# Attention followed by a token-mixing layer on one core: x transposed by DMA in six batches, attention in half groups, and products of zeros while TensorE waits

## The chip, the cores and the metric

One core of a Trainium2 chip. The metric is the device time of one execution in microseconds (us). Most executions of one kernel agree within 0.3%. Below, a "batch" is one of the eight batch entries that the program computes in a row.

Engines in the profile: PE is TensorE's matmuls, PEld its weight loads, DVE is VectorE, ACT is ScalarE, POOL is GpSimd, SP is SyncE. SPq and ACTq are the DMA queues that SP and ACT issue to. PEclk is the granted TensorE clock as a share of full speed.

## The reference, cut to what matters

```python
# q: 8 batches x 16 heads x 384 x 64;  k, v: 8 x 4 x 384 x 64  (4 query heads share one k/v head)
scores = (q @ k.T) / 8 ; attn = softmax(scores)
x   = (attn @ v), heads side by side              # per batch 384 x 1024
wq  = x @ w_q ; wk = x @ w_k                      # 384 x 64 each
W   = (wq @ wk.T) / 8                             # 384 x 384
out = relu(W @ x) @ w_out                         # 384 x 1024 per batch, float32
```

## The kernel before, cut to what the change touches

All matmuls are bf16. Per batch there are 18 score pairs (each followed by one exp of 128x1024 on ACT), six attention groups of two halves, and then a chain: x is transposed to xT, xT times (w_q, w_k) gives wT ("wqk", 8 products of 384 columns), `wk_tr`, `mix_c` (wk times x), `mix_m` (wq times that, relu), and 48 products of the output projection, `po`. A scheduler in Python, with a clock for each engine (`clk`) and times at which things are thought to be ready (`ready`), decides when the program is built in which order the instructions are emitted. On the chip each engine runs them in that fixed order. So where an estimate in `ready` is wrong, an engine stands and waits.

```python
def load(b):                                     # a batch's loads, float32, 2.36 MB, on SP's queue
    ...
    else:
        ld(kraw, k, 0, 4)                        # 384 KB
        ld(qraw, q, 0, half)                     # 768 KB
        ld(qraw, q, half, Hq)                    # 768 KB
        ld(vraw, v, 0, 4)                        # 384 KB

def attend(b, g):                                # one attention group, both halves: two banks
    ...
    ready["X", b, c, kp] = done
    if b > 0 and c < C - 1 and kp == KP - 1:     # C = 3: pieces 0 and 1 of x go by DMA,
        x_tr_dma(b, c)

def x_tr_dma(b, c):
    x_open(b)
    xn = xnats[b].rearrange("p c h d -> p c (h d)")
    nc.sync.dma_start_transpose(out=xTs[b][:, :, c, :], in_=xn[:, c, :])
    ready["T", b, c] = when(("X", b, c, 0), ("X", b, c, 1)) + 4500   # assumed landing, ns

def x_tr(b, c):                                  # piece 2, and all of batch 0: 8 transposes on TensorE
    ...
    for dc in range(DC):
        nc.tensor.transpose(out=ps[:, dc, :], in_=xn[:, c, dc * P:(dc + 1) * P], identity=ident)
    nc.vector.tensor_copy(out=xTs[b][:, :, c, :], in_=ps)

def after_s(b, s):                               # what is started after score pair s of batch b
    n = b + 1
    if b == 0 or n >= B:
        return
    if s == 0:
        load(n)                                  # the next batch's loads
    elif s == 5:
        cast(n)
        start_tr(n)
    elif s in (9, 11, 13, 15):
        tr_dma(n, (s - 9) // 2)                  # K and Q of the next batch, transposed by DMA
```

Scores run about one batch ahead of the chain. That is why the loads of batch b+2 are issued about when x of batch b is complete: they hang on the first score pair of batch b+1.

The softmax here doesn't subtract the row's maximum and nothing guards it: scores larger than these inputs give would overflow.

## Time and profile before

| | before |
|---|---|
| time, median of 3 runs | 223.95 us (223.94 to 224.87) |
| span of the profiled run | 221.7 us |
| busy: PE, DVE, ACT, POOL | 92%, 65%, 64%, 24% |
| first projection product starts | 44.94 us |
| last matmul ends, then tail | 217.44 us, 4.3 us |

The page's busy line, its groups, the windows, the timelines and the landings are in the prediction below. A group's columns are line, engine, operation, output and inputs, sizes, count; then busy us and mean ns of one; then the idle time of the engine just before these instructions.

```profile
PE 87%; ACT 4%; DVE 4%; issue 2%; DMA 1%; ACTq 0%
...
L328 PE MATMUL bank<-xT,wqk_sb 128*128 128x384 bf16 x64 | 11.8, 327 | 0.0
```

The chain runs over TensorE for 87% of the span and over DMA for 1%. The step wqk, which reads xT, never waits (0.0).

### The profile page before, as it was taken

Reading aid. Unit: us, or ns where it says so; the run is one execution under the profiler, and the core shown is the slowest. Engines: PE = TensorE matmul, PEld = TensorE weight load, DVE = VectorE, ACT = ScalarE, POOL = GpSimd, SP = SyncE. Lnnn points to the kernel's source line nnn. Section 1 sums busy time; section 2 is a strip of 40 time slices with the busy share of each in tenths; the row PEclk is TensorE's granted clock in tenths of the full one; section 3 lists DMA queues with packets and bytes.
Section 4 is the critical chain, followed back from the end, with each engine's and each line's share of the span. In section 5 each row is a group of like instructions: output and inputs, shape, how many; then the busy total and the mean of one; then the engine's idle time right before and its main releaser. Section 6 shows DMA issues by size and latency. Waiting matters only on the chain.

```text
span 221.7 us, 5331 instructions
## 1 busy us (share of the span) xinstructions
PE 204.7 (92%) x2164; PEld 106.5 (48%) x2164; DVE 144.1 (65%) x363; ACT 140.9 (64%) x146; POOL 52.3 (24%) x97
## 2 busy tenths in 40 slices
PE   1686899799999999999999999999999998999992
PEld 0264575446454645454546454644554553434440
DVE  2363776946786678768866687665876578475341
ACT  3588988978877887788788868787778730000000
POOL 1378757304400440027004400260000000000000
PEclk9999999999999999999999999999999999999999
DMA  6999999899869978899999997998422420332433
GB/s 166 329 326 263 418 368 290 159 232 353 132 186 237 348 98 220 196 324 242 154 272 348 147 223 194 336 209 163 142 95 52 142 95 3 146 138 95 191 143 143
DMA packets 71400, 46.09 MB, mean 208 GB/s; under 512 B 42704, under 2 KB 67280, under 8 KB 71376
## 3 DMA queue, kind: packets, MB, share of 16 engines
q1 hardware_dynamic: 71376, 45.75, 78.0%
q8 instruction: 17, 0.28, 0.5%
q14 instruction: 7, 0.06, 0.1%
HBM read 23.59 MB, written 12.58 MB: 163 GB/s over the span
## 4 chain that ended last, share of the span: by engine, by line
PE 87%; ACT 4%; DVE 4%; issue 2%; DMA 1%; ACTq 0%
PE bank L405 39%; PE bank L277 16%; PE sc L247 16%; PE bank L328 5%; ACT pt L251 4%; PE bank L359 3%; PE bank L381 2%; PE bank L319 2%; PE bank L212 2%; DMA kraw<-in_k_dram 1%; DVE xnat L286 1%; DVE wT L334 1%; DVE wq L336 0%; PE bank L346 0%; PE bank L196 0%
## 5 line engine op out<-in xcount | busy, mean ns | idle before, releaser
L251 ACT ACTIVATE pt<-sc 128x1024 bf16<-128x1024 f32 x144 | 139.2, 1021 | 34.9 <-PE sc L247 34.8
L405 PE MATMUL bank<-wout_sb,msb 128*128 128x512 bf16 x384 | 94.6, 380 | 0.3 <-DVE msb L386 0.3
L405 PEld LDWEIGHTS <-msb 128*128 128x128 bf16 x384 | 33.9, 97 | 45.9 <-issue 14.5
L247 PE MATMUL sc<-QT,KT 64*128 64x512 bf16 x288 | 46.2, 389 | 5.1 <-ACT pt L251 3.9
L277 PEld LDWEIGHTS <-pt 128*128 128x128 bf16 x1152 | 41.3, 98 | 14.0 <-issue 4.6
L414 DVE COPY osb<-bank 128x512 f32<-128x512 f32 x48 | 33.0, 688 | 21.8 <-PE bank L405 21.6
L277 PE MATMUL bank<-vext,pt 128*128 128x65 bf16 x1152 | 45.4, 194 | 1.4 <-ACT pt L251 1.4
L286 DVE TENSOR_TENSOR xnat<-bank,rcp 128x256 bf16<-128x256 f32 x96 | 40.8, 425 | 3.3
L386 DVE TENSOR_SCALAR msb<-bank 128x384 bf16<-128x384 f32 x64 | 32.3, 550 | 3.9 <-PE bank L381 3.7
L146 POOL CAST qb<-qraw 128x768 bf16<-128x768 f32 x30 | 24.0, 829 | 19.4 <-DMA qraw<-in_q_dram 15.7
L285 DVE RECIPROCAL rcp<-bank 128x4 f32<-128x4 f32 x96 | 17.0, 177 | 17.5 <-PE bank L277 17.1
L247 PEld LDWEIGHTS <-KT 64*128 64x128 bf16 x288 | 12.9, 94 | 25.8 <-issue 21.8
L141 POOL CAST kb<-kraw 128x192 bf16<-128x192 f32 x30 | 9.2, 350 | 65.9 <-DMA kraw<-in_k_dram 65.9
L328 PE MATMUL bank<-xT,wqk_sb 128*128 128x384 bf16 x64 | 11.8, 327 | 0.0
L381 PE MATMUL bank<-wq,Csb 64*128 64x384 bf16 x32 | 10.4, 326 | 0.1
L381 PE MATMUL bank<-wT,Csb 64*128 64x384 bf16 x32 | 10.4, 326 | 0.0
L363 DVE CAST Csb<-bank 128x512 bf16<-128x512 f32 x8 | 5.5, 692 | 7.5 <-PE bank L359 7.5
L334 DVE CAST wT<-bank 128x384 bf16<-128x384 f32 x8 | 4.5, 558 | 7.7 <-PE bank L328 7.7
L320 DVE COPY xT<-bank 128x1024 bf16<-128x1024 bf16 x10 | 6.7, 688 | 3.6 <-PE bank L319 3.6
L586 POOL CAST wout_sb<-wld 128x1024 bf16<-128x1024 f32 x8 | 8.1, 1042 | 3.9 <-DMA wld<-in_moe_w_out_dram 3.9
L328 PEld LDWEIGHTS <-wqk_sb 128*128 128x128 bf16 x64 | 5.7, 98 | 5.6 <-issue 1.9
L154 POOL CAST vext<-vraw 128x384 bf16<-128x384 f32 x16 | 7.8, 510 | 0.0
(30 smaller groups left out, 55.2 us busy)
## 6 DMA issues: line engine op xcount, KB each, us to landing
out_dram<-osb SPq DMA_DIRECT2D x24, 512.0 KB, 2.8
qraw<-in_q_dram SPq DMA_DIRECT2D x15, 768.0 KB, 8.7
wld<-in_moe_w_out_dram SPq DMA_DIRECT2D x4, 1024.0 KB, 8.2
kraw<-in_k_dram SPq DMA_DIRECT2D x7, 384.0 KB, 4.3
vraw<-in_v_dram SPq DMA_DIRECT2D x7, 384.0 KB, 9.2
qraw<-in_q_dram SPq DMA_DIRECT2D x1, 512.0 KB, 6.0
kraw<-in_k_dram SPq DMA_DIRECT2D x2, 192.0 KB, 4.2
vraw<-in_v_dram SPq DMA_DIRECT2D x2, 192.0 KB, 6.8
```

Of the source, the lines that this page charges most:

```text
L141: eng.tensor_copy(out=nats[b][0][:, kp, :, u, :], in_=raws[b][0][:, 2 * kp + u])
L146: eng.tensor_copy(out=nats[b][1][:, :, kp, :, u, :].rearrange("p c i d -> p i c d"), in_=raws[b][2][:, h0:h0 + G])
L247: nc.tensor.matmul(out=ps[:, u, :], lhsT=KT[lo:hi, kp * C + kc, :], rhs=QT[lo:hi, t0:t0 + G, :].rearrange("k i p -> k (i p)"), start=True, ...
L251: nc.scalar.activation(out=pt.rearrange("k u i p -> k u (i p)"), in_=ps, func=AF.Exp, scale=attn_scale)
L277: nc.tensor.matmul(out=outs[u][:, i * DE:i * DE + D + 1], lhsT=tiles[kc][:, u, i, :], rhs=vext[:, 2 * kp + u, kc, :D + 1], start=(kc == 0) ...
L285: nc.vector.reciprocal(out=rcp, in_=avv[:, :, D])
L286: nc.vector.tensor_tensor(out=xout[:, u], in0=avv[:, :, :D], in1=rcp.to_broadcast([P, G, D]), op=ALU.mult)
L328: nc.tensor.matmul(out=ps, lhsT=wqk_sb[:, dc, :], rhs=xT[:, dc].rearrange("d c p -> d (c p)"), start=(dc == 0), stop=(dc == DC - 1))
L381: nc.tensor.matmul(out=bank_ps[i][:, :S], lhsT=Csb[lo:hi, j * P:(j + 1) * P], rhs=w[lo:hi, :], start=True, stop=True)
L386: nc.vector.tensor_scalar_max(out=msb[:, dc, :], in0=bank_ps[i][:, :S], scalar1=0.0)
L405: nc.tensor.matmul(out=ps, lhsT=msbs[b][:, dc, c * P:(c + 1) * P], rhs=wout_sb[:, dc, half * NH:(half + 1) * NH], start=(nd == 0), stop=(n ...
L414: nc.vector.tensor_copy(out=osb[:, half * NH:(half + 1) * NH], in_=ps)
```

## The change

Its intent: take the last x transposes off TensorE, which is the bound; let attention start with one free bank; give scores precedence in the first two batches; and keep the array warm with products of zeros, which nobody reads, where the scheduler sees TensorE wait there. The last output tile is stored in three pieces.

```diff
+    EAGER = 1
+    DMA_TR = 5500
+    FILL = 109
...
+    def keep_busy(ns):
+        free, i = bank()
+        if free > clk["pe"]:
+            return
+        for _ in range(int((ns - 70) // FILL)):
+            nc.tensor.matmul(out=bank_ps[i][:, :256], lhsT=idle[:, :P], rhs=idle, start=True, stop=True)
...
-    def attend(b, g):
+    def attend(b, g, u):                  # one half u of a group, one bank
...
-        if b > 0 and c < C - 1 and kp == KP - 1:
+        if x_by_dma(b, c) and kp == KP - 1:
             x_tr_dma(b, c)
+
+    def x_by_dma(b, c):
+        return b > 0 and (c < C - 1 or b < B - 1)
...
-        ready["T", b, c] = when(("X", b, c, 0), ("X", b, c, 1)) + 4500
+        ready["T", b, c] = when(("X", b, c, 0), ("X", b, c, 1)) + DMA_TR
...
+        last = b == B - 1 and c == C - 1
+            if last:                      # the last tile: 512 + 256 + 256 columns, on two queues
+                (nc.sync if n0 % NH == 0 else nc.scalar).dma_start(out=dst[:, n0:n1], in_=osb[:, n0:n1])
...
-            cands.append((s0 + 30, 7, go_s))
+            cands.append((s0, 0, go_s) if state["S"][0] <= EAGER else (s0 + 30, 7, go_s))
...
+        keep_busy(stall)
...
+    keep_busy(26 * FILL)                  # at the start, ahead of the first transposes
+    keep_busy(900)
```

More of the change, by code (lines that the diff above doesn't have):

```diff
@@ L70 @@
     wqk_sb = consts.tile([P, DC, 2 * Dh], BF16, name="wqk_sb")
+    idle = consts.tile([P, 256], BF16, name="idle")
     vexts = [consts.tile([P, Hkv, C, DE], BF16, name=f"vext{i}") for i in range(3)]
@@ L179, in tr_dma @@
             for kp in range(KP):
-                ready["K", b, kp] = clk["pe"] + 4500
+                ready["K", b, kp] = clk["pe"] + DMA_TR
         else:
@@ L185, in tr_dma @@
             for kp in range(KP):
-                ready["Q", b, kp, c] = clk["pe"] + 4500
+                ready["Q", b, kp, c] = clk["pe"] + DMA_TR
     def tr_k(b, kp0, kp1):
@@ L257, in scores @@
         ready["P", b, s] = done
-    def attend(b, g):
+    def attend(b, g, u):
         kp, c = groups(b)[g]
         vext = vexts[b % 3]
-        if g == 0:
+        if g == 0 and u == 0:
             xnats[b] = x_p.tile([P, C, Hq, D], BF16, name="xnat", bufs=3)
-        xnat = xnats[b]
-        tiles = [pts.pop((b, C * g + kc)) for kc in range(C)]
-        h0 = 2 * kp * G
-        xout = xnat[:, c, h0:h0 + 2 * G, :].rearrange("p (u i) d -> p u i d", u=2)
-        if NWIDE:
-            _, at = wide()
-            outs = [wide_ps[at][:, u, :] for u in range(2)]
-        else:
-            two = [bank(u)[1] for u in range(2)]
-            outs = [bank_ps[i] for i in two]
-        for u in range(2):
-            for i in range(G):
-                for kc in range(C):
-                    nc.tensor.matmul(out=outs[u][:, i * DE:i * DE + D + 1],
-                                     lhsT=tiles[kc][:, u, i, :],
-                                     rhs=vext[:, 2 * kp + u, kc, :D + 1],
-                                     start=(kc == 0), stop=(kc == C - 1))
-            if NWIDE:
-                continue
-            avv = outs[u][:, :G * DE].rearrange("p (i e) -> p i e", i=G)
-            rcp = small_p.tile([P, G], F32, name="rcp", bufs=4)
-            nc.vector.reciprocal(out=rcp, in_=avv[:, :, D])
-            nc.vector.tensor_tensor(out=xout[:, u], in0=avv[:, :, :D],
-                                    in1=rcp.to_broadcast([P, G, D]), op=ALU.mult)
-            done = bank_free[two[u]] = on("dve", 665, pe(370))
-        if NWIDE:
-            avv = wide_ps[at][:, :, :G * DE].rearrange("p u (i e) -> p u i e", i=G)
-            rcp = small_p.tile([P, 2, G], F32, name="rcp")
-            nc.vector.reciprocal(out=rcp, in_=avv[:, :, :, D])
-            nc.vector.tensor_tensor(out=xout, in0=avv[:, :, :, :D],
-                                    in1=rcp.to_broadcast([P, 2, G, D]), op=ALU.mult)
-            done = wide_free[at] = on("dve", 935, pe(750))
-        ready["X", b, c, kp] = done
-        if b > 0 and c < C - 1 and kp == KP - 1:
@@ new lines, in attend @@
+        tiles = [pts[b, C * g + kc] for kc in range(C)]
+        at = bank()[1]
+        ps = bank_ps[at]
+        for i in range(G):
+            for kc in range(C):
+                nc.tensor.matmul(out=ps[:, i * DE:i * DE + D + 1], lhsT=tiles[kc][:, u, i, :],
+                                 rhs=vext[:, 2 * kp + u, kc, :D + 1],
+                                 start=(kc == 0), stop=(kc == C - 1))
+        avv = ps[:, :G * DE].rearrange("p (i e) -> p i e", i=G)
+        rcp = small_p.tile([P, G], F32, name="rcp", bufs=4)
@@ new lines, in attend @@
+        nc.vector.reciprocal(out=rcp, in_=avv[:, :, D])
+        h0 = (2 * kp + u) * G
+        nc.vector.tensor_tensor(out=xnats[b][:, c, h0:h0 + G, :], in0=avv[:, :, :D],
+                                in1=rcp.to_broadcast([P, G, D]), op=ALU.mult)
+        bank_free[at] = on("dve", 665, pe(370))
+        if u == 0:
+            return
+        for kc in range(C):
+            pts.pop((b, C * g + kc))
+        ready["X", b, c, kp] = bank_free[at]
+        if x_by_dma(b, c) and kp == KP - 1:
@@ L413, in po @@
         osb = osbs[b, c]
-        nc.vector.tensor_copy(out=osb[:, half * NH:(half + 1) * NH], in_=ps)
+        dst = out[b].rearrange("(p c) n -> c p n", c=C)[c]
+        last = b == B - 1 and c == C - 1
+        for n0 in range(half * NH, (half + 1) * NH, NH // 2 if last and half else NH):
+            n1 = n0 + (NH // 2 if last and half else NH)
+            nc.vector.tensor_copy(out=osb[:, n0:n1], in_=ps[:, n0 - half * NH:n1 - half * NH])
+            if last:
+                (nc.sync if n0 % NH == 0 else nc.scalar).dma_start(out=dst[:, n0:n1], in_=osb[:, n0:n1])
         bank_free[i] = on("dve", 690, end)
-        if half == 1:
-            nc.sync.dma_start(out=out[b].rearrange("(p c) n -> c p n", c=C)[c], in_=osb)
-    state = {"S": (0, 0), "A": (0, 0)}
+        if half == 1 and not last:
+            nc.sync.dma_start(out=dst, in_=osb)
+    state = {"S": (0, 0), "A": (0, 0, 0)}
     prep = []
@@ L454, in cand_a @@
     def cand_a():
-        b, g = state["A"]
+        b, g, u = state["A"]
         if b == B:
             return None
-        return max(when(*[("P", b, C * g + kc) for kc in range(C)]), ready["V", b],
-                   wide()[0] if NWIDE else bank(1)[0])
+        return max(when(*[("P", b, C * g + kc) for kc in range(C)]), ready["V", b], bank()[0])
     def go_a():
-        b, g = state["A"]
-        attend(b, g)
-        if g + 1 == C * KP:
+        b, g, u = state["A"]
+        attend(b, g, u)
+        if u == 0:
+            state["A"] = (b, g, 1)
+        elif g + 1 == C * KP:
             chain_open(b)
-            state["A"] = (b + 1, 0)
+            state["A"] = (b + 1, 0, 0)
         else:
-            state["A"] = (b, g + 1)
+            state["A"] = (b, g + 1, 0)
     def chain_open(b):
@@ L472, in chain_open @@
         for c in range(C):
-            if b == 0 or c == C - 1:
+            if not x_by_dma(b, c):
                 todo.append((lambda c=c: when(("X", b, c, 0), ("X", b, c, 1)), lambda c=c: x_tr(b, c), 1))
@@ L476, in chain_open @@
         todo.append((lambda: when(("W", b)), lambda: wk_tr(b), 1))
-        todo.append((lambda: when(("N", b)), lambda: mix_c(b), 1))
+        todo.append((lambda: when(("N", b)), lambda: mix_c(b), 1, "tiled"))
         for j in range(DC // 2):
-            todo.append((lambda: when(("C", b), ("W2", b)), lambda j=j: mix_m(b, j), 2))
+            todo.append((lambda: when(("C", b), ("W2", b)), lambda j=j: mix_m(b, j), 2, "tiled"))
         chains[b] = todo
@@ L484, in cand_chain @@
     def cand_chain(b):
-        at, _, width = chains[b][0]
-        if chains.get(b - 2) or (width == 2 and any(job[0] <= b - 2 for job in bulk)):
+        at, _, width = chains[b][0][:3]
+        if chains.get(b - 2) or (len(chains[b]) == DC // 2 and any(job[0] <= b - 2 for job in bulk)):
             return INF
@@ L519, in step @@
             t = cand_chain(b)
-            row = todo[0][2] == 2
             prio = 3
-            if row and pair is not None and pair < now + 1200:
+            if todo[0][-1] == "tiled" and pair is not None and pair < now + 1200:
                 prio = 6
@@ L542, in step @@
                 todo = chains[b]
-                if todo and todo[0][2] == 2 and cand_chain(b) <= clk["pe"] + 20:
+                if todo and todo[0][-1] == "tiled" and cand_chain(b) <= clk["pe"] + 20:
                     todo.pop(0)[1]()
@@ L548, in step @@
         return True
+    nc.vector.memset(idle, 0.0)
     load(0)
@@ L604 @@
         pass
-    assert state["A"] == (B, 0) and not bulk and not prep
+    assert state["A"] == (B, 0, 0) and not bulk and not prep
 _INS = ['q', 'k', 'v', 'moe_w_q', 'moe_w_k', 'moe_w_out']
```

## The prediction

> **What bounds the kernel now.** I read the page first (busy shares, groups), then the engines in two windows, then TensorE's timeline, then the DMA queue's timeline with the landing of single transfers.
>
> ```profile
> PE 204.7 (92%) x2164; PEld 106.5 (48%) x2164; DVE 144.1 (65%) x363; ACT 140.9 (64%) x146; POOL 52.3 (24%) x97
> ...
> L251 ACT ACTIVATE pt<-sc 128x1024 bf16<-128x1024 f32 x144 | 139.2, 1021 | 34.9 <-PE sc L247 34.8
> L405 PE MATMUL bank<-wout_sb,msb 128*128 128x512 bf16 x384 | 94.6, 380 | 0.3 <-DVE msb L386 0.3
> ...
> L319 PE MATMUL bank<-ident,xnat 128*128 128x128 bf16 x80 | 5.8, 220 | 0.0
> ```
> ```profile
> 0.00:44.94 44.94, 32.85 (x446) 20.33 (x446) 26.10 (x76) 34.38 (x37) 25.61 (x47) 1.00 1.03 289
> ...
> 44.94:217.45 172.51, 171.81 (x1721) 86.19 (x1719) 117.34 (x287) 106.55 (x110) 26.68 (x50) 1.00 0.74 189
> ```
>
> The second window (columns: PE, PEld, DVE, ACT, POOL, clock, DMA share, GB/s) opens at the first output-projection product and ends with the last matmul. TensorE is busy 171.8 of its 172.5 us: that part is bound by what TensorE is given. The first 45 us are not: TensorE is idle 12.1 us there, ACT 10.6, and the DMA engines are full (share 1.03). The last matmul ends at 217.44, the span at 221.7: a tail of 4.3 us.
>
> Durations of matmuls overlap, so I price by start to start:
>
> ```profile
> 48.07 1.24 PE L405 MATMUL bank<-wout_sb,msb 128*128 128x512 bf16 x5
> 49.24 0.61 PE L247 MATMUL sc<-QT,KT 64*128 64x512 bf16 x4
> 49.78 0.62 PE L319 MATMUL bank<-ident,xnat 128*128 128x128 bf16 x8
> 50.24 0.81 PE L405 MATMUL bank<-wout_sb,msb 128*128 128x512 bf16 x3
> ```
>
> Eight x transposes cost 0.46 us. The same view elsewhere gives 0.216 for a 512-column product or a pair of 64-row score products, 0.76 for 24 attention products, 1.32 for the 8 of the x-times-w_q,w_k step ("wqk" below), 0.65 for the six of mix_c, 0.163 for a mix_m pair. The program's own counts after the first projection product sum to 157.15 us at these prices, with 134 changes between full, row-split and column-split arrays. (172.5 - 0.7 idle - 157.15) / 134 = 0.109 us per change of array form.
>
> The view that decides my prediction is the DMA queue in the steady part:
>
> ```profile
> 65.08 1.23 SPq L310 DMA_TRANSPOSE xT<-xnat  x1
> 66.37 1.32 SPq L183 DMA_TRANSPOSE QT<-qb  x1
> 67.74 0.57 SPq L117 DMA_DIRECT2D kraw<-in_k_dram  x1
> 68.36 1.17 SPq L117 DMA_DIRECT2D qraw<-in_q_dram  x2
> 69.56 2.00 SPq L117 DMA_DIRECT2D vraw<-in_v_dram  x1
> 71.76 1.26 SPq L417 DMA_DIRECT2D out_dram<-osb  x1
> ```
> Of the last two issues, the time to landing (last column, us):
> ```profile
> out_dram<-osb SPq DMA_DIRECT2D x1, 512.0 KB, 8.3
> vraw<-in_v_dram SPq DMA_DIRECT2D x1, 384.0 KB, 9.2
> ```
> An output store lands in 2.8 us by the page's median, but the one issued right behind a batch's loads took 8.3: it landed at 80.1, after vraw at 78.8. A transpose behaves alike. The loads of batch 2 ended with vraw, issued at 30.04; the x transpose issued at 36.08 came behind them:
> ```profile
> vraw<-in_v_dram SPq DMA_DIRECT2D x1, 384.0 KB, 9.6
> ```
> ```profile
> xT<-xnat SPq DMA_TRANSPOSE x1, 4.4
> ```
> They landed at 39.6 and 40.5; the median x transpose takes 3.2. So what is issued behind a batch's four loads lands some 0.9 us after the last of them, and vraw lands 11.0 to 11.9 us after the issue of kraw (five batches: 45.72, 67.74, 91.31, 111.86, 135.47).
>
> **What the Trainium skill says.** "DMA: Bandwidth & Descriptors", section "Queues, rings and completion order": SP owns one row of rings, and each DMA engine consumes its ring in order. The trace agrees (80.1 after 78.8; 40.5 after 39.6). "TensorEngine Tiling (Array Packing)", section "Key Properties": changing the tiling mode drains TensorE; here 0.109 us a time. "TensorE: Matmul & The Clock Gate", Part 1 (the clock gate): the array runs at half rate until it was busy for about 3.4 us, and falls back after a comparable idle time. The trace agrees on the first half though its clock column reads 1.00: the attention products at 11.3 go 9 in 0.5 us, from 11.8 on 9 in 0.25 us. Falling back has no case in this trace after the start.
>
> **The change, part by part.** I built the changed program and read only its order of instructions.
>
> (1) Six batches (1 to 6) lose 8 transposes on TensorE: 6 x 0.46 = 2.8 us off the bound, and 6 DVE copies of 0.69 that were hidden. (2) The order after the first projection product has 142 changes of form, not 134: +0.9. Three score pairs (0.65) and one attention group (0.76) have moved ahead of it. Its priced sum is 153.0 + 142 x 0.109 = 168.5, with about 0.5 of stalls 169.0, for 172.5: -3.5 us. (3) Half groups need one bank and not two, but no wait for a bank shows before; they cost no extra product or DVE instruction: 0. (4) In batches 0 and 1 scores are issued singly as soon as a slot is free. ACT's idle gaps of 0.2 to 0.7 us after 11 us sum to 4.0; most should go. Against it, single pairs mean 68 changes of form in place of 36 before the first projection product: +3.5 us of TensorE time where it has little slack from the 16th exp on. (5) 91 products of zeros. The first 25 run cold, 256 columns at half of 0.42 (a cold pair at 6.54) = 0.21 us, from about 0.95, as estimate until 5.4 to 6.3 us, where the K transposes began at 4.19. What follows them is warm, so the first exp moves from 7.18 to about 7.9. (6) K and Q of batch 2 are cast until 40.1, when their loads allow (DMA-bound), so batch 2's first scores cannot start before about 44. I get the first projection product at 46.5 with 39 score pairs done (before: 44.94 with 36): +1.6 us. (7) The last tile is stored in three pieces, the last of 128 KB for 512: its 1.3 us of data become 0.3; less another issue, -0.9.
>
> If this were all: -3.5 + 1.6 - 0.9 = -2.8, or 221.1 us.
>
> (8) What the transposes wait for. In the changed queue order the new transpose of each batch b (its third piece) stands right behind the four loads of batch b+2; before, an output store stood there, for which nobody waits. TensorE's wqk of batch b, in fixed order, does wait for it.
> Batch 1: Q transposes of batch 2 are issued at 40.13 as before, then one x and one Q transpose of 1.3 each; kraw at about 45.35, x landed 11.2 + 0.9 later, 57.45. TensorE comes to that wqk 6.71 priced us after the first projection product: 53.2. It stalls 4.25 us.
> Batches 2 to 5: from the end of the fourth attention group, the queue issues an x transpose (+1.0), a Q transpose (+1.3), then an output store that waits for its projection half and DVE's copy, then kraw. By the order, kraw goes out 6.1, 4.1, 6.5 and 4.05 us after that group; the transpose behind the loads lands 12.5 us later (11.6 + 0.9): 18.6, 16.6, 19.0, 16.55. TensorE's work from that group to wqk is, for batch 3: 30 projection products 6.48, 12 score pairs 2.59, 3 mix_m pairs 0.49, 96 attention products 3.04, 14 changes 1.53 = 14.1 (13.9, 14.1, 14.1, 14.9 for the four). Stalls: 4.7, 2.5, 4.9, 1.6, sum 13.7. Batch 6 has no loads behind which to stand.
> Sum: 221.1 + 4.25 + 13.7 = 239.0.
>
> As the landing may be some 0.6 us sooner than I price it, five times, I take **236 us**.
>
> **Rivals.** (A) The transposes slip past the loads and land in the 5.5 us that the kernel's new constant assumes: 221.1, within 2%. For: the schedule was evidently shaped on that, and wqk was moved 7 us behind the sixth group. Against: both landings shown above. (B) They lag, but about 2 us less than I price (the engines of one load end unevenly): stalls 2.2, 2.7, 0.5, 2.9, 0 = 8.3, so 229.5. (C) The products of zeros hold up the start more than they warm: the first exp a further us late. Worth nothing in my picture, as the first wqk stall at 57.45 is set by the loads and swallows any start; under (A) it would be +1. (D) Stalls over 3.4 us let the array fall back to half rate; each such case would cost about half of 3.4, 1.7 us: up to +5 for three.
>
> **Range and chances.** Between (B) and the full sum with a part of (D) lies most weight: 227 to 241 holds it 8 times in 10. Slower needs only 4.5 us over 223.95, that is 7.3 of the 18 us of stalls: 0.84. Within 2%: mainly (A), 0.11. Faster by over 2% needs (A) and a start 1.7 us better than I work out: 0.05.
>
> **What would show it.** TensorE's waits should have wqk waiting for the DMA xT<-xnat, some five times, 2 to 5 us each, and little else new; the x transposes' landing should split into about 3 us and 8 to 10 us (third piece of batches 1 to 5). The page's PE share should fall to about 87%. Each batch from 2 to 5 should take 23.5 to 27 us, not 22. If those landings stay under 6 us and TensorE runs through, step (8) is wrong and 221 is right. Step (1) shows in 32 x transposes for 80; step (5) in the first exp at 7.5 to 8.2; step (7) in a tail of 3.4 us.

## The result, and the profile after

| | before | after |
|---|---|---|
| time, median of 4 runs each | 224.35 us (223.94 to 224.87) | 249.07 us (248.19 to 250.09) |
| ratio | | 1.1102, 95% from 1.1043 to 1.1161 |
| span of the profiled run | 221.7 us | 248.3 us |
| mean granted clock | 0.998 | 0.952 |
| last matmul ends, then tail | 217.44, 4.3 us | 244.8, 3.5 us |

Ratios, here and below, are the mean time of one kernel's fast runs over the mean time of the other's of the same rounds; they are not quite the ratio of the medians quoted. The change made the kernel slower by 11%. The prediction had the direction right and the size wrong: 249 lies above its range of 227 to 241.

The page of the changed kernel: busy line, two rows of the span in 40 slices (each digit a tenth), the chain that ended last, and the group of wqk.

```profile
PE 219.5 (88%) x2179; PEld 112.9 (45%) x2207; DVE 141.7 (57%) x359; ACT 140.5 (57%) x146; POOL 52.3 (21%) x97
...
PE   8999999965999299993999479997999999999994
...
PEclk9999999996899869998999959999999999999999
...
PE 59%; DMA 29%; SPq 4%; DVE 3%; POOL 2%; issue 2%; DVEq 0%
...
L331 PE MATMUL bank<-xT,wqk_sb 128*128 128x384 bf16 x64 | 16.8, 423 | 20.4 <-DMA xT<-xnat 20.4
```

The row PE has a dip every four to five slices (a slice is 6.2 us), and the row PEclk has a dip under each of the first four or just behind it. The chain that ended last now runs over DMA for 29% of the span. The group of wqk tells both halves of the loss: it sat idle for 20.4 us until x's transposes landed, and the same 64 products were busy for 16.8 us where they took 11.8 before, 423 ns each for 327.

TensorE's timeline of the changed kernel (start, duration, what ran, and in brackets the idle time just before and what ended it), in batches 1 and 5:

```profile
58.72 2.72 PE L331 MATMUL bank<-xT,wqk_sb 128*128 128x384 bf16 x8 [5.14 <-DMA xT<-xnat]
...
170.75 1.47 PE L331 MATMUL bank<-xT,wqk_sb 128*128 128x384 bf16 x8 [1.72 <-DMA xT<-xnat]
```

Batches 2, 3 and 4 read 2.74 us after a wait of 4.91, 2.72 after 4.35, and 2.72 after 4.27. So four waits of over 4 us are each followed by products at half their speed, and one wait of 1.72 us is not. Windows of the changed kernel around batch 1 show it directly (columns: us, PE busy with count, granted clock, DMA share, GB/s):

```profile
53.60:58.70 5.10, 0.00 (x0) 0.90 1.23 228
58.70:60.70 2.00, 1.98 (x7) 0.50 0.01 1
...
63.70:64.70 1.00, 1.00 (x16) 0.61 0.50 201
```

TensorE does nothing while the DMA engines are full (share 1.23), and when x has landed it runs at clock 0.50. The third window's mean of 0.61 puts the return to full speed at about 64.5, as (1.00 - 0.61) / 0.50 = 0.78 of it is at half rate. Half rate thus held for 5.8 us of work here. By the clock record of the same trace it was 4.6, 3.2 and 6.0 us in batches 2 to 4.

Why x came late is read in SP's DMA queue (start and duration of an issue, then line, operation, tile), with the landing of the transpose (last column, us from issue) behind it:

```profile
46.31 0.58 SPq L129 DMA_DIRECT2D kraw<-in_k_dram  x1
...
48.13 2.58 SPq L129 DMA_DIRECT2D vraw<-in_v_dram  x1
50.81 6.02 SPq L313 DMA_TRANSPOSE xT<-xnat  x2
```
```profile
xT<-xnat SPq DMA_TRANSPOSE x1, 7.8
```

The first of the two x transposes was issued at 50.81, right behind the four loads of batch 3 (46.31 to 50.71), and landed at 58.6. In batches 2 to 5 the third piece took 8.5, 8.7, 7.2 and 6.8 us to land. In batch 6, which has no loads ahead of it, wqk did not wait.

### The profile page after: what moved, and what is told of

It reads as the page before. It is cut to its first block, busy times and chain, and to the rows that moved or that the text cites. A ratio compares the mean times of both kernels' runs of the same rounds, so it can differ in the third digit from the quotient of the medians.

```text
span 248.3 us, 5402 instructions
## 1 busy us (share of the span) xinstructions
PE 219.5 (88%) x2179; PEld 112.9 (45%) x2207; DVE 141.7 (57%) x359; ACT 140.5 (57%) x146; POOL 52.3 (21%) x97
## 4 chain that ended last, share of the span: by engine, by line
PE 59%; DMA 29%; SPq 4%; DVE 3%; POOL 2%; issue 2%; DVEq 0%
PE bank L408 29%; DMA xT<-xnat 16%; PE sc L259 9%; PE bank L282 9%; DMA qraw<-in_q_dram 8%; PE bank L331 6%; SPq L129 4%; DMA vraw<-in_v_dram 4%; PE bank L384 2%; PE bank L362 2%; DMA QT<-qb 2%; DVE msb L389 1%; DVE osb L421 1%; PE bank L349 1%; POOL qb L158 1%
## 5 line engine op out<-in xcount | busy, mean ns | idle before, releaser
L408 PE MATMUL bank<-wout_sb,msb 128*128 128x512 bf16 x356 | 92.1, 383 | 1.8 <-issue 1.0
L259 PE MATMUL sc<-QT,KT 64*128 64x512 bf16 x288 | 48.1, 394 | 1.0 <-DMA QT<-qb 0.6
L282 PEld LDWEIGHTS <-pt 128*128 128x128 bf16 x1152 | 41.9, 98 | 14.8 <-issue 8.9
L421 DVE COPY osb<-bank 128x512 f32<-128x512 f32 (+1 forms) x49 | 33.1, 677 | 23.7 <-PE bank L408 21.6
L282 PE MATMUL bank<-vext,pt 128*128 128x65 bf16 x1152 | 46.2, 194 | 0.2 <-issue 0.2
L331 PE MATMUL bank<-xT,wqk_sb 128*128 128x384 bf16 x64 | 16.8, 423 | 20.4 <-DMA xT<-xnat 20.4
L158 POOL CAST qb<-qraw 128x768 bf16<-128x768 f32 x30 | 24.0, 829 | 17.9 <-DMA qraw<-in_q_dram 12.6
L259 PEld LDWEIGHTS <-KT 64*128 64x128 bf16 x288 | 12.0, 94 | 23.0 <-issue 19.2
L331 PEld LDWEIGHTS <-wqk_sb 128*128 128x128 bf16 x64 | 7.2, 118 | 27.4 <-issue 18.5
L117 PE MATMUL bank<-idle 128*128 128x256 bf16 x91 | 15.6, 315 | 1.0 <-DVE idle L562 1.0
L117 PEld LDWEIGHTS <-idle 128*128 128x128 bf16 x91 | 9.0, 112 | 6.4 <-issue 3.6
```

Of the source, the lines that this page charges most:

```text
L117: nc.tensor.matmul(out=bank_ps[i][:, :256], lhsT=idle[:, :P], rhs=idle, start=True, stop=True)
L158: eng.tensor_copy(out=nats[b][1][:, :, kp, :, u, :].rearrange("p c i d -> p i c d"), in_=raws[b][2][:, h0:h0 + G])
L259: nc.tensor.matmul(out=ps[:, u, :], lhsT=KT[lo:hi, kp * C + kc, :], rhs=QT[lo:hi, t0:t0 + G, :].rearrange("k i p -> k (i p)"), start=True, ...
L282: nc.tensor.matmul(out=ps[:, i * DE:i * DE + D + 1], lhsT=tiles[kc][:, u, i, :], rhs=vext[:, 2 * kp + u, kc, :D + 1], start=(kc == 0), sto ...
L331: nc.tensor.matmul(out=ps, lhsT=wqk_sb[:, dc, :], rhs=xT[:, dc].rearrange("d c p -> d (c p)"), start=(dc == 0), stop=(dc == DC - 1))
L408: nc.tensor.matmul(out=ps, lhsT=msbs[b][:, dc, c * P:(c + 1) * P], rhs=wout_sb[:, dc, half * NH:(half + 1) * NH], start=(nd == 0), stop=(n ...
```

## The experiments

Edits are against the changed kernel, except where it says otherwise. The first theory: the loads ahead of x's third piece hold it back, and TensorE waits for it. Its rivals: the cost lies in the other parts (zeros, half groups, single scores); the order within the one queue, not the bytes, holds x back; and, for the excess over the prediction, half rate against longer waits.

### x_on_pe: only the x transposes put back on TensorE

```diff
     def x_by_dma(b, c):
-        return b > 0 and (c < C - 1 or b < B - 1)
+        return b > 0 and c < C - 1
```

> The whole change, but the third x piece of batches 1 to 6 is transposed on TensorE again, as before. Theory (x behind the loads): the five long waits of the x-times-w step are gone and the array stays warm, so 249 falls to 223 to 225, about the kernel before: the 2.8 us of TensorE time that the transposes cost are back and cancel the small gain of the rest. Rival (half groups, single scores or zeros did the harm): stays above 235.

Measured: 222.41 us (222.26 to 222.99), ratio to before 0.9925 (0.9899 to 0.9951). That is just under the range expected. There is no wait for xT, and the clock is 0.998. So everything else in the change is together a small gain, and the whole loss of about 25 us belongs to the x transposes, 249.07 - 222.41 = 26.7 us with what follows from them.

### only_x_dma: this part alone, put into the kernel before

```diff
-        if b > 0 and c < C - 1 and kp == KP - 1:
+        if b > 0 and (c < C - 1 or b < B - 1) and kp == KP - 1:
             x_tr_dma(b, c)
...
-            if b == 0 or c == C - 1:
+            if b == 0 or (c == C - 1 and b == B - 1):
```

> The kernel before with one part of the change alone: the third x piece of batches 1 to 6 by DMA (whole attention groups, pairs of scores, no zeros). Theory: it alone does the harm, 243 to 255 us, with about five waits for xT of 4 us or more. Rival (the parts do it together): below 235.

Measured: 257.62 us (two runs, 256.68 and 258.56), ratio 1.149 (1.1427 to 1.1553), a little above what was expected. TensorE's waits (us in total, times, longest):

```profile
PE bank L328 <- DMA xT<-xnat: 14.1, 3, 5.0
PE bank L328 <- issue: 12.6, 2, 6.7
```

Both lines are idle time ahead of wqk, 26.7 us in five cases; for two of them the profile names no releaser. The part alone costs more than the whole change. Its schedule still assumes a landing of 4.5 us, not 5.5, so wqk stands earlier in TensorE's order and waits longer; this reason was not tried separately.

### loads_after_x: the same transposes, issued ahead of the loads

```diff
     def after_s(b, s):
...
-        if s == 0:
+        if s == 0 and b == 1:
             load(n)
...
     def go_a():
...
             chain_open(b)
+            if 0 < b < B - 2:
+                load(b + 2)
```

> The whole change with the x transposes by DMA kept, but the four loads of batch b+2 (b = 1 to 5) are issued right behind batch b's third x transpose instead of ahead of it. TensorE's order is unchanged. Theory: that transpose lands in 3 to 4 us, TensorE never waits for it, 220 to 222.5 us. Rival (the transposes are late because the DMA engines are short of capacity, whatever the order): waits of 2 us or more for xT remain, above 230. Second rival: the loads, now 3 us later, make K and Q late and TensorE waits for those instead: 225 to 235.

Measured: 220.01 us (219.71 to 220.14), ratio 0.9811 (0.9787 to 0.9834). SP's queue and TensorE in batch 1 of this kernel:

```profile
47.41 1.23 SPq L313 DMA_TRANSPOSE xT<-xnat  x1
48.69 0.57 SPq L129 DMA_DIRECT2D kraw<-in_k_dram  x1
```
```profile
53.34 1.46 PE L331 MATMUL bank<-xT,wqk_sb 128*128 128x384 bf16 x8 [0.16 <-issue]
```

The x transpose now goes out 1.3 us before kraw; it lands in 4.9 us (3.1 and 3.2 in the next two batches), and wqk starts at 53.34 without a wait for x, where the changed kernel had 58.72 at half speed. PE is busy 96% of the span. Nothing but the order of x and the loads changed, and 29 us went: the first theory holds, that the loads ahead of x hold it back.

### warm: the waits kept, the array kept busy in them

```diff
     def wqk(b):
...
+        if 1 <= b <= 4:
+            for _ in range(36):
+                nc.tensor.matmul(out=bank_ps[i][:, :256], lhsT=idle[:, :P], rhs=idle, start=True, stop=True)
```

> The whole change, with 36 more products of zeros (3.9 us warm) put ahead of the x-times-w step of batches 1 to 4, where TensorE waits 4.3 to 5.1 us. The wait for the transpose itself stays as it was. Theory (each such wait lets the array fall to half rate, which costs about 2.2 us four times): 249 falls by 8 to 10 us, to 239 to 241, and the 8 products of that step take 1.3 us instead of 2.6 in each batch. Rival (the long step is slow because of late data, not the clock): 249 unchanged.

Measured: 240.88 us (239.77 to 241.32), ratio 1.075 (1.0719 to 1.0781), clock 0.997. TensorE's timeline in batch 1:

```profile
53.16 4.09 PE L331 MATMUL bank<-idle 128*128 128x256 bf16 x36 [0.16 <-issue]
...
58.09 1.46 PE L334 MATMUL bank<-xT,wqk_sb 128*128 128x384 bf16 x8 [0.84 <-DMA xT<-xnat]
```

The products of zeros fill the wait, wqk begins as late as before (58.09), but runs at full speed: 1.46 us and not 2.72 (326 ns a product over all batches, as in the kernel before). This separates the two costs of one late transpose. The wait itself remains; half rate is gone and with it 249.07 - 240.88 = 8.2 us, some 2.05 us for each of four waits. In batch 3 wqk follows the zeros with no wait: x landed at 108.61 and wqk began at 109.58, where it began 0.04 to 0.14 us after the landing in batches 1, 2 and 4. So the zeros ran over by some 0.8 us there, and half rate alone is nearer 9.0.

### loads_on_act: the loads on a queue of their own

```diff
-            nc.sync.dma_start(out=dst[:, a:z, c0:c1],
+            (nc.scalar if b >= 3 else nc.sync).dma_start(out=dst[:, a:z, c0:c1],
```

> The whole change, x transposes where they are, but the loads of batches 3 to 7 are issued by ScalarE on its own queue, so the third x transpose no longer stands behind them in the same queue while the same 16 DMA engines move the same bytes. Theory (order within one queue): it lands in 3 to 5 us instead of 8 to 9, and TensorE's 20 us of waits for xT go below 3. Rival (shared engines, whatever the queue): it still lands after 7 us or more and the waits stay above 10 us. The time alone does not decide, as ScalarE spends some 2 to 4 us a batch on issuing: 221 to 232 by the theory, above 240 by the rival.

Measured: 248.12 us (two runs, 246.76 and 249.48), ratio 1.1082 (1.1018 to 1.1147). The landing of batch 2's third x piece, issued on SP at 75.62, just after the four loads on ACT (73.32 to 75.52; last column, us):

```profile
xT<-xnat SPq DMA_TRANSPOSE x1, 8.5
```

With no load in its queue, x still lands in 8.5 us (9.4 and 8.8 in batches 1 and 3), no sooner than behind the loads in one queue (7.8, 8.5 and 8.7). Counted from the issue of kraw, it lands after 10.9 to 12.6 us in batches 1 to 5 (mean 11.6), for a mean of 12.5 in the changed kernel. So the order in one queue explains little of the delay. The Trainium skill, "DMA: Bandwidth & Descriptors", section "Issuing engines are not separate DMA queues", says that DMAs end up on the same 16 DMA engines whichever engine started them, and interleave; this run agrees as far as the landing goes.

The packets of this trace show where the time goes. Two windows behind that issue, 76.8 to 80.1 us and 80.4 to 83.0 (columns: queue, packets, MB, share of 16 engines; q10 is ACT's queue, q1 SP's):

```profile
q10 hardware_dynamic: 1526, 1.15, 109.9%
q1 hardware_dynamic: 3, 0.00, 0.0%
...
q10 hardware_dynamic: 877, 0.67, 76.5%
q1 hardware_dynamic: 879, 0.23, 38.5%
```

The first packet of x comes at 80.1, 4.5 us after its issue, and from then on the two queues get the same number of packets (256 bytes each for x, 768 for the loads). In the changed kernel x's first packet comes 4.9 us after its issue in the same batch (78.57 to 83.4); with the loads issued behind x (`loads_after_x`) it comes after 1.2 us (68.31 to 69.5). So most of the delay is a late start, in its own queue as in the shared one. What holds up that start, no run here tells.

The time must be read with care. It is as long as the changed kernel's, but for another reason: no wait for xT appears. TensorE now waits for ACT, which issues the loads between its exps:

```profile
PE sc L259 <- ACT pt L263: 18.5, 6, 3.9
```
ACT stood 4.31 us, until 50.74, while it issued four loads. Four of the five waits of over 3 us that this caused (3.2 to 3.9 us) were followed by clock 0.50. So the landings decide between the two readings of the queue; the run's time does not.

### half_loads: fewer bytes ahead of x

```diff
-            ld(qraw, q, half, Hq)
+            if b < 3:
+                ld(qraw, q, half, Hq)
...
-            h0 = (2 * kp + u) * G
+            h0 = (2 * (kp if b < 3 else 0) + u) * G
```

From batch 3 on only half of q is loaded and is used twice: a wrong computation.

> The whole change, but of q only half the heads are loaded for batches 3 to 7, and both halves of Q are cast from them: a wrong result on purpose, every instruction else as it was. A batch's loads are then 1.57 MB and not 2.36. If the x transpose is late because it comes after those bytes (at some 0.34 MB per us, 0.79 MB are 2.3 us), it lands in about 6 us instead of 8.5, each wait shrinks by about 2.3 us (sum near 9 to 10 from 20.4), and the waits become too short to let the array fall to half rate: 227 to 235 us. If something else than bytes holds the transpose up (a fixed turn-round of the queue or of the transposes), the waits stay near 20 and the time near 249.

Measured: 227.51 us (two runs, 227.34 and 227.67), ratio 1.0153 (1.0128 to 1.0178), clock 0.992. Its wait for xT:

```profile
PE bank L332 <- DMA xT<-xnat: 4.6, 4, 1.6
```

Batch 2's third x piece was issued at 72.03 and took 7.0 us to land. From the issue of kraw (69.58) to the landing of x it is 9.4 us, where the changed kernel has 12.7 (74.37 to 87.1). About half of these 3.3 us is that x was issued sooner behind kraw (2.45 us for 4.20), with one load less issued ahead of it; the rest is the quicker landing (7.0 us for 8.5). With 1.57 MB ahead of x in place of 2.36 the waits for x fell from 20.4 to 4.6 us, the longest from 5.1 to 1.6, and after none of these did the clock fall. (It did fall once, for 3.4 us, after a wait of 2.3 us for a Q transpose at 42.6.) Less is left than the 9 to 10 us that I had expected. Whether a smaller batch of loads also lets other transfers land sooner was not tried. As the order was kept and one load of each batch taken away, it is what stands ahead that counts; bytes, packets and the number of loads went down together, and this run does not separate them.

### The other parts, on top of loads_after_x

All of these have the loads behind x and no wait for xT worth naming. `la_no_zeros`: no product of zeros.

```diff
     def keep_busy(ns):
 
+        return
```

> The version with the loads behind the x transpose (220.0), without any products of zeros. Theory of the prediction (the start is set by the loads of batch 2 and swallows what zeros cost or gain): within 0.7 us of 220.0, though the first exp moves back from 8.0 to 7.2 us. Rival 1 (zeros keep the array warm and earn their place): 221 to 223. Rival 2 (they hold up the start): 218.5 to 219.2.

Measured: 218.92 us (218.53 to 220.46), ratio 0.9776 (0.9751 to 0.9801). With the zeros it was 0.9811 (0.9787 to 0.9834). The intervals overlap: the zeros gain nothing, and perhaps cost some 0.8 us. That is the range of the second rival; the theory's range, within 0.7 us of 220.0, is missed by 0.4. The first exp begins at 7.10 us without them, at 8.00 with them, at 7.18 in the kernel before. This is the fastest version found, 2.2% faster than the kernel before and 12% faster than the changed one by medians (218.92 / 249.07 = 0.879).

`la_late_zeros`: no zeros but 16 ahead of batch 2's first scores, where `la_no_zeros` waits 1.9 us for a Q transpose and its profiled run, its slowest, lost its clock.

```diff
     def go_s():
         b, s = state["S"]
+        if (b, s) == (2, 0):
+            i = bank()[1]
+            for _ in range(16):
+                nc.tensor.matmul(out=bank_ps[i][:, :256], lhsT=idle[:, :P], rhs=idle, start=True, stop=True)
```

> The version with the loads behind the x transpose and no zeros (218.9), with 16 products of zeros (1.7 us) in one place alone: ahead of batch 2's first scores, where TensorE waits 1.9 us for Q and the array ran at half rate afterwards in the profiled run. If that wait costs the warm array in most runs, 217.0 to 218.2; if in few, within 0.5 us of 218.9, with a narrower spread.

Measured: 219.85 us (219.01 to 220.5), ratio 0.9807 (0.9784 to 0.9829). No gain over `la_no_zeros`, and above both ranges expected.

`la_pairs`: scores in pairs in the first two batches too, as before.

```diff
-    EAGER = 1
+    EAGER = -1
```

> The version with the loads behind the x transpose (220.0), but scores of batches 0 and 1 issued in pairs again (as in the kernel before). If single scores earn what ScalarE's idle gaps cost (4.0 us in the kernel before), 222 to 224. If the start is set by the loads of batch 2, within 0.7 us of 220.0.

Measured: 220.84 us (220.36 to 221.43), ratio 0.9865 (0.984 to 0.9891), just outside the interval of `loads_after_x`: single scores gain some 0.8 us by the medians, which is between the two ranges expected.

`la_whole`: both halves of a group together, with two free banks asked for.

```diff
-        return max(when(*[("P", b, C * g + kc) for kc in range(C)]), ready["V", b], bank()[0])
+        return max(when(*[("P", b, C * g + kc) for kc in range(C)]), ready["V", b], bank(1)[0])
...
-        attend(b, g, u)
-        if u == 0:
-            state["A"] = (b, g, 1)
-        elif g + 1 == C * KP:
+        attend(b, g, 0)
+        attend(b, g, 1)
+        if g + 1 == C * KP:
```

> The version with the loads behind the x transpose (220.0), but both halves of an attention group issued together and only when two banks are free. The prediction gave the half groups 0: within 0.5 us of 220.0. Rival (they let a half slip in where one bank is free): 221 or more.

Measured: 219.53 us (219.19 to 220.2), ratio 0.9811 (0.9786 to 0.9836). Half groups are worth nothing here.

`la_old_tail`: the last tile stored whole.

```diff
-        last = b == B - 1 and c == C - 1
+        last = False
```

> The version with the loads behind the x transpose (220.0) with the last tile stored in one piece, as before. The prediction gave the three pieces 0.9 us: 220.6 to 221.2. Rival (issuing two more stores costs what the shorter last one gains): 219.6 to 220.3.

Measured: 221.14 us (220.54 to 223.69), ratio 0.9903 (0.9863 to 0.9942). The split store gains about 1.1 us by the medians (221.14 - 220.01) and 0.9% by the ratios; two of the six runs here had a lower clock (0.987 and 0.988), which raises the ratio. The traces show the tails themselves: 4.4 us here, 3.5 in `loads_after_x`.

## Why the prediction was right and wrong, point by point

**Right: what bounds, what would wait, and where.** wqk waits for the DMA of x in batches 1 to 5 and not in batch 6, and there is little else new. The third pieces landed in 6.8 to 8.7 us (I had said 8 to 10). In batch 1, kraw was issued at 46.31 (predicted 45.35) and x landed at 58.6 (57.45). The PE share is 88% (87), the tail 3.5 us (3.4). One sign was missed: from one wqk to the next, batches 2 to 5 took 28.4, 28.7, 28.0 and 26.9 us, where I had said 23.5 to 27 (22 before).

**Right: rivals (A) and (B) don't hold, and the rest of the change is a small gain.** Without late transposes the change gives 220.01 us (predicted 221.1). Of its steps: (1) fewer transposes on TensorE, predicted 2.8 us, is 222.41 - 220.01 = 2.4, though the order of the loads differs too; (3) half groups, predicted 0, is 0; (7) the split store, predicted 0.9, is 0.9 by the tails and about 1.1 by the medians. (5) The zeros delay the first exp more than I said, to 8.81 us in the changed kernel, and to 8.00 with the same start in `loads_after_x`; the same 25 products took 5.52 and 4.73 us there. That was swallowed (going by `la_no_zeros`, all but some 0.8 us at most), as rival (C) says: the first projection product came at 47.06 and 46.67, for 46.5 predicted.

**Wrong: two terms of the sum.** From the medians:

| | predicted, us | measured, us | from |
|---|---|---|---|
| kernel before | 223.95 | 224.3 | |
| rest of the change | -2.8 | -4.3 | `loads_after_x` 220.01 less before 224.3 |
| waits for x | +15 (18.0 less 3) | +20.9 | `warm` 240.88 less 220.01; the trace sums 20.4 |
| half rate behind the waits | 0 (rival D) | +8.2 | changed kernel 249.07 less `warm` |
| sum | 236 | 249.1 | |

*The step that failed first* is the last one ahead of the prediction's number: "As the landing may be some 0.6 us sooner than I price it, five times, I take 236". This discount had no line of the profile behind it. From the issue of kraw to the landing of x it took 12.3, 12.7, 13.4, 11.9 and 12.3 us in batches 1 to 5, 12.5 in the mean, where the working had priced 12.1 once and 12.5 four times. In the first batch x landed 1.15 us later than priced, most of it because kraw went out 0.96 later. The waits came out at 5.14, 4.91, 4.35, 4.27 and 1.72 against the priced 4.25, 4.7, 2.5, 4.9 and 1.6. The third was mis-sized by the most, 1.85 us.

*The step that failed second* is rival (D), half rate after a long wait. I listed it, priced it at 1.7 us a case, and kept it out of the 236. By my own stalls three waits were over 3.4 us, so by the rule that I quoted it was due, not a possibility: it would have added 5. It came in four batches, at 2.05 us each. Together with the undiscounted waits the prediction's own terms would have given 239 + 5 = 244, outside its own upper end. The size of the price was short too: I took half of 3.4 us, and the clock stayed at 0.50 for 3.2 to 6.0 us of work in the four batches.

*The mechanism was right in its effect; its reason is at best a part.* I argued from the order of one ring. `loads_on_act` shows that a transpose in another queue is as late. It is late where 2.36 MB of loads were issued just before it, in whichever queue; `half_loads` shows that behind a smaller batch of loads it comes sooner, `loads_after_x` that ahead of them it comes in 3 to 5 us. The packets show that the larger part is a late start (4.5 to 4.9 us from issue to the first packet in batch 2, for 1.2), and the rest slower going once it has started (3.1 us from its first packet to its last in `loads_on_act`, 1.4 in `loads_after_x`). Why the start is late stays open.

*One reading of the trace was wrong.* "The attention products at 11.3 go 9 in 0.5 us, from 11.8 on 9 in 0.25 us" takes the counts of a windows view, which count each product in every window that it overlaps. By their starts the products from 11.3 follow each other every 0.054 us until 12.5; the 24 products took 1.43 us, and the next 24, at 14.46, took 0.91. So there is a slow start, as the prediction says, but it ends at about 12.5, not at 11.8, and nothing in the forecast rests on it.

## What to carry to other kernels

Before work is moved from the bound engine to DMA, look in the queue's timeline at what stands ahead of the new transfer at that moment: against x on TensorE (222.41 us), the same transposes lost 26.7 us behind a batch's prefetch and gained 2.4 us ahead of it. What an engine waits for soon goes out before what is needed a batch later, and another queue was no substitute for that order here. When a long wait of TensorE is predicted, add the time that it then runs at half speed to the sum, as a term and not as a rival. In the traces, once TensorE had started, 13 of its 14 waits of 3.2 us or more were followed by clock 0.50; so were single waits of 2.31 us (`half_loads`) and 1.89 us (`la_no_zeros`), but not those of 1.72, 1.57 and 1.54 us (changed kernel, `half_loads`, `x_on_pe`).

## What the Trainium skill lacked or had wrong

- "TensorE: Matmul & The Clock Gate", Part 1, gives about 3.4 us of work until the array is back at full rate; after the four long waits it took 5.8, 4.6, 3.2 and 6.0 us at clock 0.50. The page's section on HAM oscillation describes this very pattern, waits for DMA of 3 to 5 us after which the work runs slow, and counts half of the slow time as lost. The prediction did not use it. What it lacks is the price of a single wait in the midst of a long kernel: here 2.05 us in the mean of four waits of 4.27 to 5.14 us (8.2 us between the changed kernel and `warm`), and nothing after a wait of 1.72 us. It also lacks the shorter waits after which the clock fell here, 1.89 and 2.31 us.
- The same page warns that recorded clock events can be unreliable, but names no record that misses the start: in the kernel before, the first record begins at 12.53 us and the column reads 1.00 from 0 on, while 24 attention products took 1.43 us at 11.32 and 0.91 us at 14.46.
- "DMA: Bandwidth & Descriptors", section "Queues, rings and completion order": each DMA engine takes turns between queues, packet by packet. The trace of `loads_on_act` agrees once x has started (879 and 877 packets in 2.6 us). What the page lacks is the late start: x's first packet came 4.5 us after its issue in a queue of its own and 4.9 behind the loads in one queue, 1.2 with no loads ahead (batch 2), so that it landed after 8.5 us in both.
- The same page, section "Issuing engines are not separate DMA queues": the time to issue is "usually small relative to the DMA itself". Here ACT stood 4.31 us for four loads, and TensorE waited 18.5 us for ACT in that run, about as much as the 20.4 us of waits for x that the move took away.
- The same page, section "Latency and other measured facts", gives a bandwidth for DMA transposes (261 GB/s, from which I estimate 1.0 us for 256 KB) but no time to landing within SBUF: 128x1024 bf16 landed in 3.0 to 3.2 us where nothing stood ahead, and the third pieces in 6.8 to 8.7 us behind a batch's loads.
- "TensorEngine Tiling (Array Packing)", section "Key Properties": names the drain at a change of tiling mode without a figure; 0.109 us a change was fitted to the kernel before.
